# Block decay of the attention state: from a TensorE sum in every chunk, instead of a copied row past the first chunk

## The chip, the core and the metric

The kernel runs on one core of a Trainium2 chip. The metric is the device time of one execution in microseconds (us). A profiled execution gives, beside its own time, the span from the first to the last instruction of the program and a trace of every engine: PE (TensorE: matmuls; its weight loads are shown as PEld), DVE (VectorE), ACT (ScalarE), POOL (GpSimd) and SP (SyncE, whose queue issues most DMAs here).

## The reference: gated linear attention, then a soft mixture of four experts

For 4 batches and 8 heads, with sequence 768 and head size 48:

```
f = 1 / (1 + exp(-f_logit))
for t in range(S):
    state = f[:, :, t, :, None] * state + k[t] (outer) v[t]
    y[t]  = q[t] @ state
x = y with heads side by side                      # (3072, 384)
p = domain_probs / (domain_probs.sum(-1) + 1e-9)   # (3072, 4)
out = sum over 4 experts e of  p[:, e] * (relu(x @ w1[e]) @ w2[e])
```

`w1[e]` is 384x1024 and `w2[e]` 1024x384.

## The kernel before

**Tiling.** The sequence is cut into 6 chunks `c` of 128 steps. In a chunk each batch `b` has one tile with time on the 128 partitions and 8 heads by 48 channels along the rows. The recurrence is done by blocks: with `g = log(1 + exp(-f_logit))` (which is minus the log of the gate) and `cs` its running sum over the 128 steps, the scores are (q times exp(-cs)) against (k times exp(cs)), masked to the lower triangle; the state at the end of the chunk is (old state + KV) times exp(-cs of the last step). This last factor, one number for each head and channel, is the block decay, `egs`. Heads are handled in pairs: 4 pairs, each with 48 + 48 channels at partitions 0 to 47 and 64 to 111 (MP = 112 partitions).

**Steps of a chunk and batch**, with their lines:

- `gate1`, `gate2` (L247, L251): two activations on ACT give `g` in bf16, for one batch in chunk 0 and for two batches together later.
- `pe_cs` (L255): one matmul with a triangle of ones gives `cs` (128x384) in PSUM. In chunk 0 alone, L258 adds four matmuls, one for each head pair: `g` of the pair (128x112) is the stationary operand and a column of ones the moving one, so that each gives a 112x1 column with the sum of `g` over the chunk.
- `exps` (L262, L264): exp(-cs) and exp(cs) into the two halves of a tile `e`. The first is written permuted, (channel, head) instead of (head, channel). In chunk 0 alone, L266 takes the exp of the four columns into `egs` (112x4).
- `dma_egs` (L271), in chunks 1 to 4: two DMAs copy the last row of exp(-cs) onto the partitions of `egs`. The permuted order makes a channel's four pairs neighbours for this copy.
- `product` (L276): q times exp(-cs) and k times exp(cs), in bf16, on DVE or POOL.
- Transposes of q and k (on PE, L285, in chunks 0 and 1; by DMA, L289, later), scores (`pe_at`, L300), mask (`ev_at`, L304), output (`pe_y`, L311 and L315), its transpose to x (L340 on PE, or L293 by DMA).
- For the next chunk: `pe_kv` (L321), `ev_kv` (L328, DVE adds KV to the state) and `state` (L335, L336, POOL: state times `egs`, and a bf16 copy).

**The experts.** For chunk `c`, the four batches' x make 512 columns. `mm_h` (L344) does three matmuls of 512 columns for each of 8 blocks of 128 hidden units; `relu` (L350 on DVE, L352 on ACT) takes them out of PSUM; `mm_o` (L356) does four matmuls of 384 columns at a time; `ev_o` (L363, L365, L367) scales by the probability and adds. PSUM has four buffers for these (`ps_m`) and four for the attention (`ps_t`).

**What sets the order.** The program's order on each engine is written by a planner, `Plan.run` (L58): a list scheduler that is given every step with assumed costs in us, priorities, what it depends on, and the buffers ("rooms") that it takes and frees; it decides also which of the allowed engines does a step. Each engine then works in that order, whatever the real times are. The attention of chunk c + 1 is planned among the experts' work of chunk c. Between chunk 0's steps on PE it writes matmuls on a constant tile (L551, "pads"). Input loads, probability loads (`load_p`, L237, one for each chunk), `egs` copies, DMA transposes and stores all stand in SP's queue; the eight weight loads (L229) are issued by POOL, the first of them after POOL's third product and after the load of k for the last batch of chunk 0.

Of the kernel before, what the change touches and what calls it, by code (L numbers as in the profile page):

```python
# [99 lines left out]
def kernel(  # L100
# [14 lines left out]
    T = 128  # L115
# [15 lines left out]
    wk = ctx.enter_context(tc.tile_pool(name="wk", bufs=1))  # L131
    PS = bass.MemoryType.PSUM
    ps = ctx.enter_context(tc.tile_pool(name="ps", bufs=1, space=PS))
    rooms = {"ps_m": 4, "ps_t": 4, "f": 4, "q": 4, "k": 4, "v": 4, "ex": 2, "gp": 4, "e": 3, "qk": 7,
             "vb": 7, "egs": 8, "QK": 2, "AT": 2, "yb": 2, "xT": 2, "h": 2, "o": 6}
    P = Plan(rooms)


# [114 lines left out]
    def pe_cs(c, b):  # L253
        g, cs = tl("gp", c, b // 2)[:, b % 2], tl("cs", c, b)
        nc.tensor.matmul(out=cs[:, 0:HD], lhsT=Ub, rhs=g[:, :, 0:D], start=True, stop=True)  # L255
        if c == 0:
            for i in range(NP):
                nc.tensor.matmul(out=cs[0:MP, HD + i:HD + i + 1], lhsT=flat(g, i)[:, 0:MP], rhs=ones, start=True, stop=True)  # L258

    def exps(c, b):  # L260
        cs, e = tl("cs", c, b), tl("e", c, b)
        nc.scalar.activation(out=e[:, 0].rearrange("t (d h) -> t h d", d=D), in_=cs[:, 0:HD].rearrange("t (i r d) -> t r i d", r=2, d=D),  # L262
                             func=AF.Exp, scale=-1.0)
        nc.scalar.activation(out=e[:, 1], in_=cs[:, 0:HD], func=AF.Exp)  # L264
        if c == 0:
            nc.scalar.activation(out=tl("egs", c, b), in_=cs[0:MP, HD:HD + NP], func=AF.Exp, scale=-1.0)  # L266

    def dma_egs(c, b):
        last = tl("e", c, b)[T - 1:T, 0].rearrange("o (d r i) -> o r d i", r=2, d=D)
        for r in range(2):  # L270
            nc.sync.dma_start(out=tl("egs", c, b)[r * P2:r * P2 + D, :], in_=last[:, r])  # L271

    def product(c, b, j, eng):
        e = tl("e", c, b)[:, j]
        e = e.rearrange("t (d r i) -> t i r d", d=D, r=2) if j == 0 else e.rearrange("t (i r d) -> t i r d", d=D, r=2)
        engines[eng].tensor_tensor(out=tl("qk", c, b)[:, j, :, 0:D].rearrange("t (i r) d -> t i r d", r=2),  # L276
                                   in0=tl("qk"[j], c, b // 2)[:, hh(b), :].rearrange("t (i r) d -> t i r d", r=2),
                                   in1=e, op=ALU.mult)

    def cast_v(c, b, eng):  # L280
        copy(eng, tl("vb", c, b), tl("v", c, b // 2)[:, hh(b), :])
# [114 lines left out]
    xdone, kvdone = {}, {}  # L396

    def attention(c, slot, gran):
        G, X, Y, GS = {}, [], [], []
        more = c < C - 1  # L400
        for b0 in range(0, B, gran):
            p, d, half = slot(b0, 0) - 0.5, 0.54 if gran == 1 else 0.84, b0 // 2
            g1 = P.add(f"gate1 {c}.{b0}", {"ACT": d}, lambda e, b0=b0: gate1(c, b0, gran), p,
                       deps=[ld[c, "f", b0]], takes=[("ex", c, b0)], frees=[("f", c, half)])
            g2 = P.add(f"gate2 {c}.{b0}", {"ACT": d}, lambda e, b0=b0: gate2(c, b0, gran), p + 0.1,
                       deps=[g1], takes=[("gp", c, half)], frees=[("ex", c, b0)])
            for b in range(b0, b0 + gran):
                G[b] = g2
        for b in range(B):
            s = lambda k: slot(b, k)  # L410
            half = b // 2
            pt_ = lambda kind, *x: ("ps_t", kind, c, b) + x
            on = lambda f, *x: (lambda e, b=b: f(c, b, *x))
            one = lambda f, *x: (lambda e, b=b: f(c, b, *x, e))
            cs = P.add(f"cs {c}.{b}", {"PE": 0.17 if c else 0.36}, on(pe_cs), s(0),
                       deps=[G[b]], takes=[pt_("cs")], lag=0.2, frees=[("gp", c, half)])
            ex = P.add(f"exps {c}.{b}", {"ACT": 0.98 if c else 1.1}, on(exps), s(0) + 0.1, deps=[cs],
                       takes=[("e", c, b)] + ([("egs", c, b)] if c == 0 else []), frees=[pt_("cs")])
            GS.append(P.add(f"egs {c}.{b}", {"DMA": 1.0}, on(dma_egs), s(3), deps=[ex], takes=[("egs", c, b)],
                            frees=[("e", c, b)], lag=2.0) if c and more else None)  # L420
            pe = {"DVE": 0.6, "POOL": 1.0} if c < 2 else {"POOL": 1.0}
            qm = P.add(f"q {c}.{b}", pe, one(product, 0), s(4) - 0.2,
                       deps=[ex, ld[c, "q", b]], takes=[("qk", c, b)], frees=[("q", c, half), ("e", c, b)])
            km = P.add(f"k {c}.{b}", pe, one(product, 1), s(4) - 0.1,
                       deps=[ex, ld[c, "k", b]], takes=[("qk", c, b)], frees=[("k", c, half), ("e", c, b)])
            vb = P.add(f"v {c}.{b}", {"ACT": 0.52, "DVE": 0.36} if c == 0 else {"POOL": 0.5, "ACT": 0.52} if c == 1 else {"POOL": 0.5}, one(cast_v), s(4),
                       deps=[ld[c, "v", b]], takes=[("vb", c, b)], frees=[("v", c, half)])
            if c < 2:
                tq = P.add(f"tpq {c}.{b}", {"PE": 0.22}, on(pe_tp, 0), s(4), deps=[qm],
                           takes=[pt_("tp")], frees=[("qk", c, b)], lag=0.2)  # L430
                tk = P.add(f"tpk {c}.{b}", {"PE": 0.22}, on(pe_tp, 1), s(4) + 0.01, deps=[km],
                           takes=[pt_("tp")], frees=[("qk", c, b)], lag=0.2)
                et = P.add(f"ev_tp {c}.{b}", {"DVE": 0.69, "ACT": 1.05}, lambda e, b=b: copy(e, tl("QK", c, b)[0:MP], tl("tp", c, b)), s(4) + 0.1,
                           deps=[tq, tk], takes=[("QK", c, b)], frees=[pt_("tp")])
            else:
                et = P.add(f"tp {c}.{b}", {"DMA": 1.8}, on(dma_tp), s(4), deps=[qm, km], takes=[("QK", c, b)],
                           frees=[("qk", c, b)], lag=2.2)
            at = P.add(f"at {c}.{b}", {"PE": 0.35}, on(pe_at), s(7), deps=[et],
                       takes=[pt_("A", 0), pt_("A", 1)], lag=0.2, frees=[("QK", c, b)])
            eA = [P.add(f"ev_at{r} {c}.{b}", {"DVE": 0.7}, on(ev_at, r), s(7) + 0.1 + 0.1 * r, deps=[at],  # L440
                        takes=[("AT", c, b)], frees=[pt_("A", r)]) for r in range(2)]
            y = P.add(f"y {c}.{b}", {"PE": 0.4 if c else 0.28}, on(pe_y), s(11), deps=eA + [vb, kvdone.get((c - 1, b))],
                      takes=[pt_("y")], frees=[("QK", c, b), ("AT", c, b), ("vb", c, b)], lag=0.2)
            Y.append(y)
            ey = P.add(f"ev_y {c}.{b}", {"ACT": 0.48, "DVE": 0.56},
                       lambda e, b=b: copy(e, tl("yb", c, b), tl("y", c, b)[:, 0:HD]), s(11) + 0.1,
                       deps=[y], takes=[("yb", c, b)], frees=[pt_("y")])
            if c < 2:
                xt = P.add(f"xt {c}.{b}", {"PE": 0.17}, on(pe_xt), s(13), deps=[ey],
                           takes=[pt_("xp")], frees=[("yb", c, b)], lag=0.2)  # L450
                xdone[c, b] = P.add(f"ev_xt {c}.{b}", {"ACT": 0.48, "DVE": 0.4},
                                    lambda e, b=b: copy(e, tl("xT", c)[:, :, b * T:(b + 1) * T], tl("xp", c, b)),
                                    s(13) + 0.1, deps=[xt], takes=[("xT", c)], frees=[pt_("xp")])
            else:
                xdone[c, b] = P.add(f"xt {c}.{b}", {"DMA": 0.9}, on(dma_xt), s(13), deps=[ey], takes=[("xT", c)],
                                    frees=[("yb", c, b)], lag=2.2)
            X.append(xdone[c, b])
        for b in range(B if more else 0):
            on = lambda f, b=b: (lambda e: f(c, b))
            pt_ = lambda kind, b=b: ("ps_t", kind, c, b)  # L460
            s15 = slot(b, 15) if c else 2 + 2 * b
            kv = P.add(f"kv {c}.{b}", {"PE": 0.22}, on(pe_kv), s15, deps=[Y[b], X[B - 1] if c == 0 else None],
                       takes=[pt_("KV")], frees=[("vb", c, b), ("qk", c, b)], lag=0.2)
            ek = P.add(f"ev_kv {c}.{b}", {"DVE": 0.74}, on(ev_kv), s15 + 0.1,
                       deps=[kv, kvdone.get((c - 1, b))], frees=[pt_("KV")])
            kvdone[c, b] = P.add(f"state {c}.{b}", {"POOL": 1.75}, on(state), s15 + 0.2,
                                 deps=[ek, GS[b]], frees=[("egs", c, b)])


    unit = [0]  # L470
# [115 lines left out]
```

## Time and profile before

| | us |
|---|---|
| median of 3 runs | 305.13 (305.03 to 305.37) |
| the profiled execution's own time | 305.37 |
| its span | 303.5 |
| PE busy | 294.5 |
| PEld busy | 170.5 |
| ACT busy | 170.7 |
| DVE busy | 137.8 |
| POOL busy | 95.7 |

What lies around the span is 305.37 - 303.5 = 1.9 us. "Busy" of PE counts from the start of a matmul to its modelled end; matmuls overlap, so the distance from one start to the next is what a matmul costs a full PE. Groups of instructions are read as: line, engine, operation, tiles written and read, shapes, count, then busy us in total, mean ns of one, and the idle time of the engine before them with what ended it. In the timeline a row has the start in us, the length in us, and then engine, line and tiles.

### The profile page before, as it was taken

The page shows a single profiled execution, that of the slowest core. Times are in us where ns is not written, and L with a number is a line of the kernel's source. Part 1 is how long each engine was busy: PE and PEld are TensorE (multiplying, and loading weights), DVE is VectorE, ACT ScalarE, POOL GpSimd, SP SyncE. Part 2 cuts the span into 40 slices and gives each one's busy share as a digit, 9 for nine tenths or more (in the row PEclk, how much of TensorE's full clock was granted, in tenths as well). Part 3 has the DMA queues.
Part 4 walks back from the last instruction along what each step waited for, and adds up shares of the span by engine and source line. Part 5 has one row for each costly group of instructions (what it writes and reads, how often), then busy time and mean ns, then how long its engine had stood idle before and what let it go on. Part 6 is the DMA issues. An engine that isn't in the chain of part 4 may idle for free.

```text
span 303.5 us, 5499 instructions
## 1 busy us (share of the span) xinstructions
PE 294.5 (97%) x2104; PEld 170.5 (56%) x2135; DVE 137.8 (45%) x272; ACT 170.7 (56%) x295; POOL 95.7 (32%) x157
## 2 busy tenths in 40 slices
PE   7899999999999999999999999999999999999995
PEld 5665555567775655455555555555555555555552
DVE  6684013788853764516555344544423443201223
ACT  5767654957865444676356475345476444475430
POOL 4585200408656237423426243522432000000000
PEclk9999999999999999999999999999999999999999
DMA  7999999955993589776997877301322201100002
GB/s 156 204 185 208 208 206 190 225 90 91 215 208 82 111 165 181 170 144 120 189 178 136 213 142 151 51 13 37 92 59 51 48 14 41 73 5 2 0 0 104
DMA packets 137210, 36.08 MB, mean 119 GB/s; under 512 B 128480, under 2 KB 135648, under 8 KB 137184
## 3 DMA queue, kind: packets, MB, share of 16 engines
q1 hardware_dynamic: 131424, 29.45, 48.8%
q0 software_dynamic: 5760, 6.29, 12.5%
q8 instruction: 16, 0.26, 0.4%
q14 instruction: 10, 0.08, 0.1%
HBM read 31.51 MB, written 4.72 MB: 119 GB/s over the span
## 4 chain that ended last, share of the span: by engine, by line
PE 90%; DMA 4%; DVE 2%; POOL 1%; issue 1%; ACT 1%; DVEq 0%; ACTq 0%; POOLq 0%
PE ps_m L356 40%; PE ps_m L344 40%; DMA w_sb<-in_moe_w_dram 3%; PE ps_t L300 2%; PE ps_t L255 1%; PE ps_t L315 1%; PE ps_t L321 1%; PE ps_t L311 1%; PE ps_t L285 1%; DMA f<-in_f_logit_dram 1%; POOL qk L276 1%; PE ps_m L551 1%; DVE qk L276 1%; DVE o L363 0%; DVE AT L304 0%
## 5 line engine op out<-in xcount | busy, mean ns | idle before, releaser
L352 ACT ACTIVATE h<-ps_m 128x512 bf16<-128x512 f32 (+1 forms) x171 | 98.4, 578 | 102.7 <-PE ps_m L344 92.5
L356 PE MATMUL ps_m<-w_sb,h 128*128 128x384 bf16 x768 | 153.0, 326 | 0.2
L344 PE MATMUL ps_m<-xT,w_sb 128*128 128x512 bf16 (+1 forms) x593 | 150.4, 362 | 1.9 <-DVE o L367 0.3
L356 PEld LDWEIGHTS <-h 128*128 128x128 bf16 x768 | 72.5, 98 | 57.4
L363 DVE SCALAR_TENSOR_TENSOR o<-ps_m,pn,o 128x384 f32<-128x384 f32 x72 | 44.4, 617 | 97.2 <-PE ps_m L356 89.8
L344 PEld LDWEIGHTS <-w_sb 128*128 128x128 bf16 x624 | 59.8, 98 | 46.9 <-issue 0.7
L276 POOL TENSOR_TENSOR qk<-q,e 128x384 bf16<-128x384 f32 x19 | 22.8, 1203 | 66.7 <-ACT e L262 66.2
L304 DVE TENSOR_TENSOR AT<-ps_t,mask 128x512 bf16<-128x512 f32 x48 | 31.1, 685 | 19.3 <-PE ps_t L300 19.2
L335 POOL TENSOR_TENSOR Sf<-Sf,egs 48x192 f32<-48x192 f32 x40 | 20.4, 510 | 47.5 <-DVE Sf L328 45.5
L350 DVE TENSOR_SCALAR h<-ps_m 128x512 bf16<-128x512 f32 (+1 forms) x37 | 20.7, 573 | 22.0 <-PE ps_m L344 19.7
L276 POOL TENSOR_TENSOR qk<-k,e 128x384 bf16<-128x384 f32 x20 | 21.3, 1064 | 20.3 <-ACT e L264 13.0
L262 ACT ACTIVATE e<-ps_t 128x384 f32<-128x384 f32 x24 | 20.7, 864 | 4.6 <-PE ps_t L255 2.4
L328 DVE TENSOR_TENSOR Sf<-Sf,ps_t 48x192 f32<-48x192 f32 x40 | 14.0, 350 | 9.4 <-PE ps_t L321 8.7
L336 POOL CAST sb<-Sf 48x192 bf16<-48x192 f32 x40 | 13.6, 339 | 2.6
L551 PE MATMUL ps_m<-busy 128*128 128x256 bf16 x71 | 13.1, 332 | 1.3 <-DVE busy L140 1.3
L365 ACT ACTIVATE o<-ps_m,pn 128x384 f32<-128x384 f32 x20 | 11.6, 581 | 3.9 <-PE ps_m L356 3.1
L264 ACT ACTIVATE e<-ps_t 128x384 f32<-128x384 f32 x24 | 13.0, 541 | 0.0
L218 DVE CAST yb<-ps_t 128x384 bf16<-128x384 f32 x16 | 8.9, 556 | 7.3 <-PE ps_t L315 6.3
L247 ACT ACTIVATE ex<-f 128x768 f32<-128x768 f32 (+1 forms) x14 | 10.5, 747 | 3.0 <-DMA f<-in_f_logit_dram 3.0
L315 PE MATMUL ps_t<-vb,AT 128*128 128x48 bf16 x192 | 11.4, 184 | 0.7 <-DVE vb L218 0.7
L315 PEld LDWEIGHTS <-AT 128*128 128x128 bf16 x192 | 9.8, 97 | 2.8 <-issue 0.9
L251 ACT ACTIVATE gp<-ex 128x768 bf16<-128x768 f32 (+1 forms) x14 | 10.5, 751 | 0.4
(50 smaller groups left out, 142.6 us busy)
## 6 DMA issues: line engine op xcount, KB each, us to landing
w_sb<-in_moe_w_dram POOLq DMA_DIRECT2D x8, 768.0 KB, 18.6
out_dram<-o SPq DMA_DIRECT2D x24, 192.0 KB, 1.9
f<-in_f_logit_dram SPq DMA_DIRECT2D x10, 384.0 KB, 4.2
k<-in_k_dram SPq DMA_DIRECT2D x10, 384.0 KB, 5.3
q<-in_q_dram SPq DMA_DIRECT2D x10, 384.0 KB, 5.3
v<-in_v_dram SPq DMA_DIRECT2D x10, 384.0 KB, 5.5
f<-in_f_logit_dram SPq DMA_DIRECT2D x4, 192.0 KB, 3.8
k<-in_k_dram SPq DMA_DIRECT2D x4, 192.0 KB, 3.9
```

The source lines that it names most:

```text
L262: nc.scalar.activation(out=e[:, 0].rearrange("t (d h) -> t h d", d=D), in_=cs[:, 0:HD].rearrange("t (i r d) -> t r i d", r=2, d=D), func=A ...
L276: engines[eng].tensor_tensor(out=tl("qk", c, b)[:, j, :, 0:D].rearrange("t (i r) d -> t i r d", r=2), in0=tl("qk"[j], c, b // 2)[:, hh(b), ...
L304: nc.vector.tensor_tensor(out=tl("AT", c, b)[:, r].rearrange("s i t -> s (i t)"), in0=tl("A", c, b, r).rearrange("s i t -> s (i t)"), in1= ...
L315: nc.tensor.matmul(out=y[:, h * D:(h + 1) * D], lhsT=AT[:, r, i, :], rhs=vb[:, h, :], start=(c == 0), stop=True, skip_group_check=True)
L328: nc.vector.tensor_tensor(out=Sf[rows, b], in0=Sf[rows, b], in1=KV[rows, :, r, :], op=ALU.add)
L335: nc.gpsimd.tensor_tensor(out=Sf[rows, b], in0=Sf[rows, b], in1=eg, op=ALU.mult)
L344: nc.tensor.matmul(out=tl("hp", c, e, fc, n0)[:, n0:n1], lhsT=w1_sb[:, e, kk, fc * 128:(fc + 1) * 128], rhs=tl("xT", c)[:, kk, n0:n1], sta ...
L350: nc.vector.tensor_relu(out=dst, in_=src)
L352: nc.scalar.activation(out=dst, in_=src, func=AF.Relu)
L356: nc.tensor.matmul(out=tl("op", c, e, nt)[:, 0:Din], lhsT=tl("h", c, e)[:, fc, nt * T:(nt + 1) * T], rhs=w2_sb[:, e, fc, :], start=(fc == ...
L363: nc.vector.scalar_tensor_tensor(out=o, in0=op, scalar=pe, in1=o, op0=ALU.mult, op1=ALU.add)
L551: nc.tensor.matmul(out=spare[:, 0:256], lhsT=busy[:, 0:128], rhs=busy, start=True, stop=True)
```

## The change

In every chunk but the last, `pe_cs` now does the four column sums and `exps` the small exp that gives `egs`, as chunk 0 did already; the copies by DMA are gone, and with them the permuted order of exp(-cs). The products read both halves of `e` in the plain order. `e` has 2 buffers instead of 3, and the output tile `o` 8 instead of 6. The costs given to the planner are changed with it, so it writes a new order for all engines. A short description that goes with the change speaks of the domain probabilities loaded and normalised chunk by chunk; the diff leaves `load_p` and `probs` as they are, and only their places in the queues are planned anew.

```diff
     rooms = {"ps_m": 4, "ps_t": 4, "f": 4, "q": 4, "k": 4, "v": 4, "ex": 2, "gp": 4,
-             "e": 3, ... "o": 6}
+             "e": 2, ... "o": 8}
...
     def pe_cs(c, b):
...
-        if c == 0:
+        if c < C - 1:
             for i in range(NP):
                 nc.tensor.matmul(out=cs[0:MP, HD + i:HD + i + 1], lhsT=flat(g, i)[:, 0:MP], rhs=ones, start=True, stop=True)

     def exps(c, b):
         cs, e = tl("cs", c, b), tl("e", c, b)
-        nc.scalar.activation(out=e[:, 0].rearrange("t (d h) -> t h d", d=D), in_=cs[:, 0:HD].rearrange("t (i r d) -> t r i d", r=2, d=D),
-                             func=AF.Exp, scale=-1.0)
+        nc.scalar.activation(out=e[:, 0], in_=cs[:, 0:HD], func=AF.Exp, scale=-1.0)
         nc.scalar.activation(out=e[:, 1], in_=cs[:, 0:HD], func=AF.Exp)
-        if c == 0:
+        if c < C - 1:
             nc.scalar.activation(out=tl("egs", c, b), in_=cs[0:MP, HD:HD + NP], func=AF.Exp, scale=-1.0)

-    def dma_egs(c, b):
-        last = tl("e", c, b)[T - 1:T, 0].rearrange("o (d r i) -> o r d i", r=2, d=D)
-        for r in range(2):
-            nc.sync.dma_start(out=tl("egs", c, b)[r * P2:r * P2 + D, :], in_=last[:, r])
-
     def product(c, b, j, eng):
-        e = tl("e", c, b)[:, j]
-        e = e.rearrange("t (d r i) -> t i r d", d=D, r=2) if j == 0 else e.rearrange("t (i r d) -> t i r d", d=D, r=2)
-        engines[eng].tensor_tensor(out=tl("qk", c, b)[:, j, :, 0:D].rearrange("t (i r) d -> t i r d", r=2),
-                                   in0=tl("qk"[j], c, b // 2)[:, hh(b), :].rearrange("t (i r) d -> t i r d", r=2),
-                                   in1=e, op=ALU.mult)
+        engines[eng].tensor_tensor(out=tl("qk", c, b)[:, j, :, 0:D], in0=tl("qk"[j], c, b // 2)[:, hh(b), :],
+                                   in1=tl("e", c, b)[:, j].rearrange("t (h d) -> t h d", d=D), op=ALU.mult)
...
-            cs = P.add(f"cs {c}.{b}", {"PE": 0.17 if c else 0.36}, on(pe_cs), s(0),
+            cs = P.add(f"cs {c}.{b}", {"PE": 0.36 if more else 0.17}, on(pe_cs), s(0),
                        deps=[G[b]], takes=[pt_("cs")], lag=0.2, frees=[("gp", c, half)])
-            ex = P.add(f"exps {c}.{b}", {"ACT": 0.98 if c else 1.1}, on(exps), s(0) + 0.1, deps=[cs],
-                       takes=[("e", c, b)] + ([("egs", c, b)] if c == 0 else []), frees=[pt_("cs")])
-            GS.append(P.add(f"egs {c}.{b}", {"DMA": 1.0}, on(dma_egs), s(3), deps=[ex], takes=[("egs", c, b)],
-                            frees=[("e", c, b)], lag=2.0) if c and more else None)
+            ex = P.add(f"exps {c}.{b}", {"ACT": 1.1}, on(exps), s(0) + 0.1, deps=[cs],
+                       takes=[("e", c, b)] + ([("egs", c, b)] if more else []), frees=[pt_("cs")])
...
             kvdone[c, b] = P.add(f"state {c}.{b}", {"POOL": 1.75}, on(state), s15 + 0.2,
-                                 deps=[ek, GS[b]], frees=[("egs", c, b)])
+                                 deps=[ek], frees=[("egs", c, b)])
```

More of the change, by code (lines that the diff above doesn't have):

```diff
@@ L133 @@
     ps = ctx.enter_context(tc.tile_pool(name="ps", bufs=1, space=PS))
-    rooms = {"ps_m": 4, "ps_t": 4, "f": 4, "q": 4, "k": 4, "v": 4, "ex": 2, "gp": 4, "e": 3, "qk": 7,
-             "vb": 7, "egs": 8, "QK": 2, "AT": 2, "yb": 2, "xT": 2, "h": 2, "o": 6}
+    rooms = {"ps_m": 4, "ps_t": 4, "f": 4, "q": 4, "k": 4, "v": 4, "ex": 2, "gp": 4, "e": 2, "qk": 7,
+             "vb": 7, "egs": 8, "QK": 2, "AT": 2, "yb": 2, "xT": 2, "h": 2, "o": 8}
     P = Plan(rooms)
@@ L398, in attention @@
     def attention(c, slot, gran):
-        G, X, Y, GS = {}, [], [], []
+        G, X, Y = {}, [], []
         more = c < C - 1
```

## The prediction, made before the changed kernel was run

> **What bounds the kernel now.** I read the page first: shares of the engines, clock, and the chain that ended last.
>
> ```profile
> span 303.5 us, 5499 instructions
> ...
> PE 294.5 (97%) x2104; PEld 170.5 (56%) x2135; DVE 137.8 (45%) x272; ACT 170.7 (56%) x295; POOL 95.7 (32%) x157
> ...
> PEclk9999999999999999999999999999999999999999
> ...
> PE 90%; DMA 4%; DVE 2%; POOL 1%; issue 1%; ACT 1%; DVEq 0%; ACTq 0%; POOLq 0%
> ```
>
> PE is busy 97% of the span at full granted clock, and 90% of the chain is PE; the next engine is at 56%. But busy PE is not yet full PE, so next come PE's waits for other engines, over the whole span:
>
> ```profile
> PE ps_t L315 <- DVE vb L218: 0.7, 1, 0.7
> ...
> PE ps_m L344 <- DVE o L367: 0.3, 1, 0.3
> PE ps_t L285 <- DVE qk L276: 0.3, 1, 0.3
> ```
>
> The first of these lies at 15 us, in the opening. From the first expert matmul at 23.04 us on, the two others are all: about 0.65 us in 276. So from there on PE is the bound in the strict sense: what is added to its queue is added to the time, and a faster ACT, DVE, POOL or SP buys at most those 0.65 us. Before 23.04 us PE is not the bound. The chain of waits, in order of time, shows what is (start, length, what):
>
> ```profile
> 13.60 1.31 POOL qk L276
> 14.91 8.08 DMA w_sb<-in_moe_w_dram
> 22.99 0.04 issue
> 23.04 0.39 PE ps_m L344
> ```
>
> POOL's third product must end before POOL issues the first weight load, the load takes 8.08 us, and the first expert matmul starts 0.05 us after it lands. Here ACT's and POOL's speed does count.
>
> **Part 1, added: four column sums in chunks 1 to 4.** 4 chunks by 4 batches are 16 groups of four matmuls (64, each with its weight load of 112 columns), on the engine that is the bound. The price is read from chunk 0, which has such groups. PE's timeline:
>
> ```profile
> 12.66 0.33 PE L255 MATMUL ps_t<-gp,Ub 128*128 128x384 bf16 x1
> 12.82 0.32 PE L258 MATMUL ps_t<-ones,gp 128*112 128x1 bf16 x4
> 13.01 0.27 PE L551 MATMUL ps_m<-busy 128*128 128x256 bf16 x1
> ```
>
> From the start of the group to the start of the next matmul: 13.01 - 12.82 = 0.19 us, with nothing waited for. 16 x 0.19 = 3.04 us. The 0.32 us of length are no price: they overlap what follows. Bounds: above, four matmuls with 112-column weights and 96 moving columns (`pe_kv`), in the steady state, take 63.58 - 63.38 = 0.20 us, 3.2 in all:
>
> ```profile
> 63.38 0.36 PE L321 MATMUL ps_t<-vb,qk 128*112 128x96 bf16 x4
> 63.58 0.81 PE L356 MATMUL ps_m<-w_sb,h 128*128 128x384 bf16 x4
> ```
>
> Below, eight matmuls with 128-column weights and 48 moving columns go in 18.16 - 17.94 = 0.22 us, that is 0.11 for four, 1.76 in all:
>
> ```profile
> 17.94 0.37 PE L315 MATMUL ps_t<-vb,AT 128*128 128x48 bf16 x8
> 18.16 0.60 PE L551 MATMUL ps_m<-busy 128*128 128x256 bf16 x4
> ```
>
> I take 3.04, the row of the very instruction. The groups in the steady state stand between the same kinds of neighbour (a 384-column L255 before, a matmul with 128-column weights behind).
>
> That the weight load sets this price is told by PEld's groups: L321 x80 at a mean of 131 ns and L258 x16 at 170 for 112 columns, against L356 x768 at 98 for 128 columns; the narrower load is the slower. The Trainium skill, "TensorE: Matmul & The Clock Gate", section "Weight-path perf modes — Fast Weight Load (FWL) and DoubleRow", has a rule for it: the fast load is on when the number of weights is 128, so 112 columns do without. Its section "LDWEIGHTS (loading the stationary operand)" then gives P / 1.2 ns for P columns, 93 ns for 112; if every load stood in the open, the 64 would cost 6.0 us and the prediction would be some 3 us higher. The group's row, 190 ns for four loads, is half of that, so the measurement decides and the sum goes by 3.04.
>
> **Part 2, in the opening: exp(-cs) in plain order.** ACT's groups:
>
> ```profile
> L262 ACT ACTIVATE e<-ps_t 128x384 f32<-128x384 f32 x24 | 20.7, 864 | 4.6 <-PE ps_t L255 2.4 <-PE ps_t L258 2.3
> L264 ACT ACTIVATE e<-ps_t 128x384 f32<-128x384 f32 x24 | 13.0, 541 | 0.0
> L266 ACT ACTIVATE egs<-ps_t 112x4 f32<-112x4 f32 x4 | 0.7, 165 | 0.0
> ```
>
> The permuted exp takes 864 ns, the plain one 541. Consecutive activations overlap: from 9.28 (L262) to 9.93 (L264) are 0.65 us, from 9.93 to 10.36 (L266) 0.43, so a plain one brings what follows on ACT forward by 0.22 us. Two lie on the chain: `exps` of batch 1 starts at 9.28 because its cs has just ended on PE, which does not move (pads stand before it, and their number, 71, is the same in the new program). From there ACT works without a hole up to `exps` of batch 2 at 12.36. Its cs ends on PE near 12.05 and stays there, since three pads from 10.97 lead up to it; brought forward by 0.22, `exps` starts at 12.14, still behind it. With its own 0.22, POOL's third product starts 0.44 us earlier, and the weight load is issued at 14.47. Its other condition, k of batch 3, had landed at 14.31. So the issue gains 0.4 us. The load of 8.08 us shares the DMA engines with inputs until 18.0, so its end gains between 0 and 0.44; nothing stands ahead of it in POOL's own queue, and DMA moved least just when it ramped up (103 GB/s between 17 and 18 us, 138 in the next, against 241 at 15 and 209 at 20), so I take 0.4. The other thing that the first expert matmul waits for, x of batch 3, is copied from 22.44 to 22.92 and must gain as much: on DVE, which runs without a hole from 9.79, the permuted q products cost 11.17 - 10.40 = 0.77 each against 16.77 - 16.30 = 0.47 for a plain one, three of them 0.9; enough. `e` with 2 buffers makes batch 2's exps wait for batch 0's products, which ended at 7.4 and 8.3: nothing.
>
> **Part 3, work that moves or goes beside PE.** ACT loses 24 x 0.323 = 7.8 us of length and gains 16 x 0.165 = 2.6; POOL's q products fall from 1203 ns toward the 1064 of k; SP loses 32 issues of a median of 578 ns (18.5 us) and the waits before them, so the loads of chunk 2 are no longer behind the copies of chunk 1's decays and start near 61 us instead of 71.6. None of this had PE waiting but for the two waits of 0.3 us, both about chunk 1, where DVE's permuted q product and an o scaling were late and where ACT was filled by chunk 2's permuted exps. In the new order chunk 2's first cs stand before the 512-column halves there, so both waits can go, and new ones can come: the stretch takes relus of 256 columns (388 ns on ACT) as fast as PE makes them. From -0.65 (both gone) to +1.0 (three waits of the largest kind, 0.35 us); I take -0.35, half gone. POOL never waited for a copied `egs` (its 45.5 us at L335 are all for DVE), so an earlier one gives nothing. The probability loads: chunk 1's is issued earlier, those of 2 and 3 one behind the other; each lands in about 2.8 us, chunks ahead of its use.
>
> The added wait is the `e` slot: `exps` of a batch waits for both products, mostly on POOL, of the batch two before. Behind it on ACT stand relus, and behind these PE, when its four `ps_m` buffers are full. The planner places exps by assumed product costs of 1.0 us, real ones take 1.06, so lateness of a tenth of a microsecond is to be expected, less than the gap of 0.7 us that ACT shows before most relus of the steady state. I cost it at nothing; without that cover it is the second rival.
>
> **Sum.** 3.04 - 0.4 - 0.35 = +2.3 us. The profiled execution, 305.37 (span 303.5 and 1.9 around it), becomes 307.7; it was the slowest of the three runs, 0.24 above the median, so against 305.13 I predict 307.4.
>
> **Rivals.**
>
> - *The opening gives nothing.* DMA is full until 18.0 us and the first weights land when the bytes are through; or x is late. For it: DMA stands at the top tenth from the second of the 40 slices to the eighth. Against: the dip between 17 and 19 us, room that an earlier issue can use. Then +3.04 - 0.35 to +3.04: 307.8 to 308.2.
> - *ACT's head is held by the `e` slot.* Decides where exps' wait exceeds the 0.7 us before relus. A product of 1.2 us late, less 0.7, in each of chunks 1 to 4: 4 x 0.5 = 2.0 on top, 309.4. Against: POOL is 32% busy.
> - *Faster: the sums hide.* If the 112-column loads slip wholly under the neighbours' streams, a group costs nothing and the opening and the freed waits remain: -0.75, 304.4. It decides below 0.75 / 16 = 0.047 us for a group. Against: 0.19 in the row above, with PE not waiting, and 0.11 even for the cheapest four.
> - *The change does not do what its short description says*: the probabilities' loads only move in the queue, which is worth nothing either way; the time is then that of parts 1 to 3.
>
> **How the numbers follow.** The forecast (+1.4 to +2.7: 306.5 to 307.8) has 0.63; no gain in the opening 0.17; the `e` slot or another new wait of that size 0.12; cheaper sums (0.11 a group, 1.76 - 0.75 = +1.0, 306.1) 0.04; hidden sums 0.04. The range, 306.2 to 308.7, holds the first two and part of the third. A measurement of this kernel tells about 0.2% (0.6 us) from no change: faster 0.03, same 0.04 (the bottom of the last two cases), slower 0.93.
>
> **What would show it.** 80 matmuls in the column-sum group, 64 of them new, at 0.18 to 0.20 us for four in the steady timeline; exp(-cs) at 541 ns; the first weight load issued near 14.5 and the first expert matmul near 22.6 us; PE's waits after it together below 1 us; the end of PE's work about 2.3 us later. It is wrong if a group costs another time among the experts' matmuls, if the first expert matmul does not move, or if PE waits for relus behind an exps.

## The result, and the profile after

The changed kernel takes 308.91 us (median of 4 runs, 308.25 to 308.97) against 305.10 for the kernel before: 3.8 us slower, a ratio of 1.0118 (95% interval 1.0101 to 1.0136). The direction was forecast; the size was not: 307.4 was predicted, with a range that ended at 308.7.

In some executions, of the kernel before and of changed ones alike, PE loses 5 to 11 us ahead of the first expert matmul to one late input load; the medians and ratios below leave them out, and where a profile fell into one (`changed_again`, `sums_128_wide`, `opening_kept`) only its rows behind the opening are read.

The page of the changed kernel: span, engines, and the head of the chain that ended last.

```profile
span 307.1 us, 5567 instructions
...
PE 297.0 (97%) x2168; PEld 173.5 (56%) x2199; DVE 134.8 (44%) x268; ACT 166.3 (54%) x316; POOL 90.5 (29%) x156
...
PE 89%; DMA 4%; SPq 3%; DVE 1%; issue 1%; DVEq 0%
```

PE remains the bound. ACT and POOL have less to do, as forecast, and it buys nothing. PE's waits for other engines, over the whole span:

```profile
...
PE ps_m L335 <- DVE o L358: 1.2, 1, 1.2
PE ps_t L306 <- DVE vb L218: 0.8, 2, 0.5
PE ps_m L335 <- DMA w_sb<-in_moe_w_dram: 0.6, 1, 0.6
PE ps_t L255 <- ACT gp L251: 0.4, 1, 0.4
```

Before, the two waits behind the opening were 0.3 us each; now there is one of 1.17, the first line, for the o scaling in DVE's queue near 83 us, and just ahead of it one of 0.14 for a relu, too short for the list; the other three lines are of the opening. The column sums, PE's groups by shape:

```profile
L258 PE MATMUL ps_t<-ones,gp 128*112 128x1 bf16 x80 | 6.8, 188 | 0.0
```

80 matmuls instead of 16, and PE waited for none of them. The opening, by the chain in order of time:

```profile
10.51 3.88 DMA k<-in_k_dram
14.39 0.30 issue
14.70 8.51 DMA w_sb<-in_moe_w_dram
23.20 0.05 issue
23.25 0.39 PE ps_m L335
```

POOL's product is no longer in it: the load of k is, which landed at 14.39, and the weight load followed 0.3 us later. So the issue came 0.21 us earlier than before (14.70 for 14.91), but the load took 8.5 us instead of 8.1, and the first expert matmul starts at 23.25 instead of 23.04. POOL's third product ended at 14.27 here; it was not what the issue waited for.

**Where the time went.** Two points of PE's timeline split the kernel: the first running sum of chunk 1 (L255), at 54.43 us before and 54.53 after, and PE's last end, 299.96 and 303.54. Up to the first point the change costs 0.10 us; from there on 249.006 - 245.532 = 3.47. The start-to-start distances of the 64 new sums add to 2.93 (28 ns for the first matmul in a group, 52 for each of the next three); PE's waits went from 0.64 (0.295 + 0.347) to 1.31 us (1.166 + 0.143), 0.67 more. 2.925 + 0.667 = 3.59; the 0.12 too much lies in PE's other work, whose order the new plan changes, and was not followed further.

### The profile page after: what moved, and what is told of

Its sections match the earlier page's. It is cut to its first block, busy times and chain, and to the rows that moved or that the text cites. A ratio compares the mean times of both kernels' runs of the same rounds, so it can differ in the third digit from the quotient of the medians.

```text
span 307.1 us, 5567 instructions
## 1 busy us (share of the span) xinstructions
PE 297.0 (97%) x2168; PEld 173.5 (56%) x2199; DVE 134.8 (44%) x268; ACT 166.3 (54%) x316; POOL 90.5 (29%) x156
## 4 chain that ended last, share of the span: by engine, by line
PE 89%; DMA 4%; SPq 3%; DVE 1%; issue 1%; DVEq 0%
PE ps_m L347 41%; PE ps_m L335 40%; SPq L222 3%; DMA w_sb<-in_moe_w_dram 3%; PE ps_t L291 2%; PE ps_t L312 1%; PE ps_t L306 1%; DMA k<-in_k_dram 1%; PE ps_t L302 1%; PE ps_t L255 1%; PE ps_t L258 1%; PE ps_t L276 1%; DVE o L354 0%; DVE psm L242 0%; DVE Sf L319 0%
## 5 line engine op out<-in xcount | busy, mean ns | idle before, releaser
L343 ACT ACTIVATE h<-ps_m 128x512 bf16<-128x512 f32 (+1 forms) x173 | 99.9, 577 | 109.7 <-PE ps_m L335 100.2
L268 POOL TENSOR_TENSOR qk<-q,e 128x384 bf16<-128x384 f32 x18 | 18.2, 1016 | 59.6 <-ACT e L262 57.3
L341 DVE TENSOR_SCALAR h<-ps_m 128x512 bf16<-128x512 f32 (+1 forms) x35 | 19.4, 567 | 23.5 <-PE ps_m L335 23.0
L356 ACT ACTIVATE o<-ps_m,pn 128x384 f32<-128x384 f32 x22 | 12.8, 580 | 5.1 <-PE ps_m L347 3.3
L262 ACT ACTIVATE e<-ps_t 128x384 f32<-128x384 f32 x24 | 11.7, 489 | 4.1 <-PE ps_t L258 4.1
L218 POOL CAST vb<-v 128x384 bf16<-128x384 f32 x18 | 9.5, 541 | 12.4 <-DMA v<-in_v_dram 7.0
L263 ACT ACTIVATE e<-ps_t 128x384 f32<-128x384 f32 x24 | 11.9, 497 | 0.0
```

The costliest lines, as they stand in the source:

```text
L268: engines[eng].tensor_tensor(out=tl("qk", c, b)[:, j, :, 0:D], in0=tl("qk"[j], c, b // 2)[:, hh(b), :], in1=tl("e", c, b)[:, j].rearrange( ...
L341: nc.vector.tensor_relu(out=dst, in_=src)
L343: nc.scalar.activation(out=dst, in_=src, func=AF.Relu)
L356: nc.scalar.activation(out=o, in_=op, func=AF.Copy, scale=pe)
```

## What ran into what near 82 us

DVE in the changed kernel, around the wait (start, length, what):

```profile
81.23 0.17 DVE L241 TENSOR_REDUCE psm<-pt 128x4 f32<-128x16 f32 x1
81.43 0.97 DVE L242 TENSOR_SCALAR psm<-psm 128x4 f32<-128x4 f32 x1
82.44 0.18 DVE L243 RECIPROCAL psm<-psm 128x4 f32<-128x4 f32 x1
82.66 0.20 DVE L244 TENSOR_TENSOR pn<-pt,psm 128x16 f32<-128x16 f32 x1
82.89 0.62 DVE L358 TENSOR_SCALAR o<-ps_m,pn 128x384 f32<-128x384 f32 x1
```

and POOL at the same time:

```profile
80.43 1.00 POOL L268 TENSOR_TENSOR qk<-q,e 128x384 bf16<-128x384 f32 x1
81.38 1.00 POOL L268 TENSOR_TENSOR qk<-k,e 128x384 bf16<-128x384 f32 x1
```

This is the normalisation of chunk 1's probabilities. Adding 1e-9 to 128x4 numbers, 0.17 us in the kernel before, took 0.97 and ended at 82.40, 0.02 after POOL's second product. In the kernel before, the same four operations stood at 80.34 to 81.17, and POOL's products of chunk 2 began at 81.86:

```profile
80.54 0.17 DVE L242 TENSOR_SCALAR psm<-psm 128x4 f32<-128x4 f32 x1
...
81.86 1.19 POOL L276 TENSOR_TENSOR qk<-q,e 128x384 bf16<-128x384 f32 x1 [0.32 <-POOL sb L336]
...
81.87 3.37 PE L344 MATMUL ps_m<-xT,w_sb 128*128 128x256 bf16 x27 [0.35 <-DVE o L367]
```

The new plan has chunk 2's exps earlier, so the two products come earlier too, between the states of chunk 1, and the normalisation now falls on them. The o scaling that frees a `ps_m` buffer stands behind it in DVE's queue, and PE waits for that buffer, for 1.17 us:

```profile
83.56 2.67 PE L335 MATMUL ps_m<-xT,w_sb 128*128 128x256 bf16 x23 [1.17 <-DVE o L358]
```

The Trainium skill, "SBUF — State Buffer", section "Who interferes with whom", says that a pair of ports is shared by VectorE and GpSimd as an exclusive lock: a DVE operation with two SBUF inputs (against a GpSimd instruction that reads SBUF), or a `tensor_scalar` in a mode that uses both ports, waits until the GpSimd instruction that holds the pair is over; a `tensor_reduce` does not. The rows agree: the `tensor_scalar` was held, and the reduce, which began at 81.23 inside POOL's first product, was not. In which mode the `tensor_scalar` ran, the trace does not show.

## The experiments

**The sums alone.** The kernel before with only this change (its `egs` still come by DMA):

```diff
-        if c == 0:
+        if c < C - 1:
             for i in range(NP):
                 nc.tensor.matmul(out=cs[0:MP, HD + i:HD + i + 1], lhsT=flat(g, i)[:, 0:MP], rhs=ones, ...)
```

> The kernel before, in its own order on every engine, with the four column sums added to the running sum's step in chunks 1 to 4; nothing reads them. Theory (each group costs PE 0.18 us wherever it stands, because from 23 us on PE is full): 16 groups, +2.9 us, 308.0 (307.7 to 308.3), with PE's waits as before. Rival (the sums are partly hidden and the rest of the 3.8 us of the change is the new order): 306.5 or less.

Measured: 307.79 us, ratio 1.0073 (1.0060 to 1.0086), some 2.2 us. The sums' distances in the trace add to 2.93, as in the changed kernel. From chunk 1's running sum to PE's end it was 248.03 - 245.53 = 2.50 us more. Of PE's two waits that had been there before, one had gone and the other was 0.10 us; the lines below are of the opening alone:

```profile
...
PE ps_m L344 <- DMA w_sb<-in_moe_w_dram: 0.8, 1, 0.8
PE ps_t L315 <- DVE vb L218: 0.7, 1, 0.7
PE ps_t L255 <- ACT gp L251: 0.5, 1, 0.5
```

What follows: work added to PE gives the others time, so part of it is paid for by PE's own waits, here some 0.5 us of the 0.64. The price of a group is what the opening's row said, wherever the group stands.

**The changed kernel without the new sums.** The counterpart: the order of the changed kernel, with `if c == 0` back in `pe_cs` and the small exp reading four columns of the running sum, so that the block decay of chunks 1 to 4 is left out.

> The changed kernel in its own order, without the column sums of chunks 1 to 4: the small exp reads four columns of the running sum instead, so the block decay of these chunks is left out. Theory: 308.9 - 2.9 = 306.0, that is 0.9 above the kernel before, which is the part of opening (+0.2) and of the waits near 82 us (+0.6). Rival (the new order costs most): 307 or more.

Measured: 305.54, ratio 1.0009 (0.9987 to 1.0031): no different from the kernel before by the times, and 1.09% below the changed kernel's 1.0118, some 3.3 us. From chunk 1's running sum to PE's end it was 245.81, 0.28 more than before and 3.20 less than the changed kernel: 2.93 of sums and, as the wait near 82 us was 0.93 instead of 1.17, 0.24 of wait. (The addition came ahead of POOL's second product here and took 0.23 us; the multiplication behind it was held, for 0.70.) So the sums are the bulk, and the new order itself costs 0.3 us, not the 0.9 expected.

**Without the addition of 1e-9.** In the changed kernel:

```diff
-        nc.vector.tensor_single_scalar(out=s, in_=s, scalar=1e-9, op=ALU.add)
```

> The changed kernel without the addition of 1e-9 to the sum of the probabilities (that part of the normalisation is left out). Theory: that operation of DVE took 0.97 us instead of 0.17 in chunk 1 because POOL's two products ran then, and PE waited for the o scaling behind it. Without it PE's wait of 1.17 us near 83 us falls to about 0.4 and the time to 308.1. Rival (DVE is held by POOL whatever it does, so the reciprocal or the multiplication takes over the wait): 308.9, and one of these at about 0.9 us.

Measured: 308.46, ratio 1.0091 (1.0077 to 1.0105), between the theory's 308.1 and the rival's 308.9. DVE's rows:

```profile
81.19 0.17 DVE L241 TENSOR_REDUCE psm<-pt 128x4 f32<-128x16 f32 x1
81.39 0.18 DVE L242 RECIPROCAL psm<-psm 128x4 f32<-128x4 f32 x1
81.61 0.77 DVE L243 TENSOR_TENSOR pn<-pt,psm 128x16 f32<-128x16 f32 x1
82.41 0.62 DVE L357 TENSOR_SCALAR o<-ps_m,pn 128x384 f32<-128x384 f32 x1
```

The rival's mechanism: the hold passed to the multiplication, with two SBUF inputs, which ended at 82.38, 0.03 after POOL's product (81.35 + 1.00). The reciprocal, begun at 81.39 inside that product, was not held. The scaling started at 82.41 instead of 82.89 only because two operations fewer stood behind the hold, and PE's wait fell to 0.73 us, not to 0.4.

**The normalisation moved away from the products.** In the changed kernel, behind the plan:

```diff
     done = P.run()
+    names = [o.name for o in done]
+    early = done.pop(names.index("probs 1"))
+    done.insert(names.index("ev_at0 1.2"), early)
```

> The changed kernel with one thing moved: DVE normalises chunk 1's probabilities before the masks of chunk 1's third batch (about 73 us) instead of after its last x (81 us), so that its operations meet none of POOL's two products; the order of PE, ACT, POOL and SP is unchanged. Theory: the o scaling behind it starts at 81.3 instead of 82.9 and PE's wait of 1.17 us near 83 us falls below 0.3: 0.9 to 1.2 us less than the changed kernel. Rival (relus on DVE and ACT are the next in line and take the wait over): no gain, 0.3 us or less.

Measured: 307.23, ratio 1.0064 (1.0051 to 1.0078), against 1.0125 (1.0110 to 1.0140) for the changed kernel in the same group of runs. From chunk 1's running sum to PE's end: 247.68 against 249.02, 1.34 us less, a little more than expected and 1.18 of it the wait; the times say 1.9, and where the rest lies was not followed. PE's list of waits has nothing of DVE's scaling any more:

```profile
PE ps_t L255 <- ACT gp L251: 1.5, 4, 0.6
...
PE ps_t L276 <- DVE qk L268: 0.8, 1, 0.8
PE ps_m L335 <- DMA w_sb<-in_moe_w_dram: 0.6, 1, 0.6
PE ps_t L331 <- ACT yb L216: 0.3, 1, 0.3
```

The addition takes 0.17 us there:

```profile
74.33 0.17 DVE L242 TENSOR_SCALAR psm<-psm 128x4 f32<-128x4 f32 x1
```

This shows what PE waited for: the same four operations on the same data, 7 us earlier, and the wait is gone. The move takes away the hold and the operations' own length at that place together. By the rows the hold is 0.97 - 0.17 = 0.80 us of the 1.17; without it, by that estimate, 0.37 would stay, as much as the 0.35 of the kernel before. The rival, relus taking the wait over, fell.

**The changed kernel again.**

> The changed kernel once more, as the base of this group of runs and as a second look at its opening. Theory: the 3.6 us are lasting parts (2.9 sums, 0.7 the wait near 83 us) and the start of the first expert matmul varies by some 0.5 us from execution to execution with the landing of the first weights, without moving the end by as much: 3.2 to 3.8 us above the kernel before. Rival (the opening's 0.2 us is a lasting loss): the first expert matmul at 23.2 again.

Measured: 308.97, ratio 1.0125 (1.0110 to 1.0140). Its profile has the wait near the o scaling again, 1.18 us, with the addition at 0.99 us, and 249.02 us from chunk 1's running sum to the end. It does not show the opening; other profiles do. First expert matmul in the old opening: 23.04 (`before`), 23.75 (`sums_alone`) and 22.69 (`before_mended`, below); in the new one: 23.25, 23.13 (`no_new_sums`), 22.65 (`no_add`), 22.59 (`probs_early`) and 23.35 (`changed_mended`, below). The 0.2 us of the changed kernel's profile are scatter, not a lasting loss.

The same profiles show what sets the issue of the first weight load. In all eight profiles with the new opening that are read there, POOL issues it 0.30 us after k of the last batch has landed (landing 14.10 to 14.45, issue 14.40 to 14.75), and its third product had ended before. In the old opening the product set it in `before` and `sums_alone` (issue 14.91 and 14.94), but not in `before_mended`, where the issue came at 14.66, again 0.30 us behind k. There PE ran its second running sum at 7.82 us in 0.32 us, against 0.53 us at 8.43 in `before`, and the third product, for all its permuted exps, ended at 14.23. So the plain exps bring the issue forward in some executions only, and then by some 0.3 us.

**The sums' weights 128 columns wide.**

```diff
-                nc.tensor.matmul(out=cs[0:MP, HD + i:HD + i + 1], lhsT=flat(g, i)[:, 0:MP], rhs=ones, ...)
+                nc.tensor.matmul(out=cs[:, HD + i:HD + i + 1], lhsT=flat(g, i), rhs=ones, ...)
```

> The changed kernel with the column sums' stationary operand 128 columns wide instead of 112 (the 16 more are the zeros that pad each head to 64), otherwise as it is. Theory (the load of 112 columns sets the 51 ns from one sum to the next, and one of 128 columns is faster, as the 28 ns between the 48-column matmuls with 128-column weights say): a group falls from 0.18 to 0.11 us, 16 x 0.07 = 1.2 us less than the changed kernel. Rival (51 ns is what a matmul of one column with its load costs, whatever the width): no difference, or 14% more per load, +0.4 us.

Measured: 307.39, ratio 1.0071 (1.0057 to 1.0084), 0.54% or 1.6 us below the changed kernel of the same group. PEld's group first in the changed kernel:

```profile
L258 PEld LDWEIGHTS <-gp 128*112 128x112 bf16 x80 | 7.6, 138 | 2.7 <-issue 0.7
```

and here, with PE's timeline below it:

```profile
L258 PEld LDWEIGHTS <-gp 128*128 128x128 bf16 x80 | 4.8, 97 | 4.8 <-issue 2.3
```

```profile
83.67 0.24 PE L258 MATMUL ps_t<-ones,gp 128*128 128x1 bf16 x4
83.77 0.38 PE L312 MATMUL ps_t<-vb,qk 128*112 128x96 bf16 x4
```

A group takes 0.10 us from start to start instead of 0.18; the distances of the 64 add to 1.65 us instead of 2.93, 25 ns where there were 52. Most of the other 0.3 us is the wait for the o scaling, which was 0.82 here: the addition came 0.04 us ahead of POOL's second product and took 0.17, and the multiplication was held instead, for 0.65. So the column sum's price is the load of its weights, and a wider load is the cheaper one. The rule cited in the prediction (the Trainium skill, "TensorE: Matmul & The Clock Gate", section "Weight-path perf modes — Fast Weight Load (FWL) and DoubleRow": the fast load is on when the number of weights is 128) agrees with this. The 93 ns for 112 columns that the formula of its section "LDWEIGHTS (loading the stationary operand)" gives are not what a load costs in the stream here, where a load and its matmul take 52.

**The opening, three ways.** First, the changed kernel with chunk 0's probabilities behind the first weight load:

```diff
-        nc.sync.dma_start(out=p_dst[:, :, c], in_=p_src[:, :, c])
+        i = nc.sync.dma_start(out=p_dst[:, :, c], in_=p_src[:, :, c])
+        if c == 0:
+            after(i, ins["w", 0])
```

> The changed kernel with chunk 0's probability load held back until the first weight load has landed. Theory: in the changed kernel the 512 short packets of that load went between the packets of the first weight load and cost it 0.4 us; without them the weights land 8.1 us after their issue, at 22.8, and the first expert matmul starts at 22.85 instead of 23.25: 308.5. Rival (the bytes of the inputs before it set the landing): 23.2 again, 308.9.

Measured: 308.98, ratio 1.0117 (1.0097 to 1.0137), no gain, although the weights landed at 22.55 and the first expert matmul started at 22.59. That the probabilities' packets had cost the weights 0.4 us is not shown, as `no_add` and `probs_early` got there with these packets in place. What the three have in common is what came after. The first running sum of chunk 1, in `probs_early` (ACT's gates and PE's sum):

```profile
52.57 0.84 ACT L247 ACTIVATE ex<-f 128x768 f32<-128x768 f32 x1 [1.74 <-DMA f<-in_f_logit_dram]
...
53.45 0.84 ACT L251 ACTIVATE gp<-ex 128x768 bf16<-128x768 f32 x1
...
54.34 0.32 PE L255 MATMUL ps_t<-gp,Ub 128*128 128x384 bf16 x1 [0.31 <-ACT gp L251]
```

PE waits for the gates, whose input had just landed. From the first expert matmul to this sum PE has 31.28 us of work (in the changed kernel, `sums_alone` and `no_new_sums` alike, with no wait there). The gates end between 53.9 and 54.8 us in the eleven profiles read there, and an earlier start of PE does not bring them forward: so a first expert matmul earlier than about 22.6 to 23.6, by where the gates end in that execution, is given back here. Even the kernel before stood at this floor:

```profile
53.53 0.84 ACT L251 ACTIVATE gp<-ex 128x768 bf16<-128x768 f32 x1
...
54.43 0.48 PE L255 MATMUL ps_t<-gp,Ub 128*128 128x384 bf16 x2
```

Its gates ended at 54.37 and its sum began 0.05 us later, the same distance as in `probs_early`, `no_add`, `p0_behind_w0` and `plain_opening`, where PE waits for them. From the first expert matmul to the sum it took 31.39 us, so 0.11 us of it was a wait that the list does not show.

Second, the opening's part of the change by itself, in the kernel before:

```diff
+        if c == 0:
+            nc.scalar.activation(out=e[:, 0], in_=cs[:, 0:HD], func=AF.Exp, scale=-1.0)
...
+        if c == 0:
+            engines[eng].tensor_tensor(out=tl("qk", c, b)[:, j, :, 0:D], in0=tl("qk"[j], c, b // 2)[:, hh(b), :],
+                                       in1=e.rearrange("t (h d) -> t h d", d=D), op=ALU.mult)
+            return
```

> The kernel before, in its own order, with exp(-cs) and its product in plain order in chunk 0 alone: the opening's part of the change by itself. Theory: the weight load is issued 0.2 to 0.4 us earlier, but PE cannot keep it, because chunk 1's running sum waits near 54.4 us for gates whose load is fixed by the weight loads: within 0.2 us of the kernel before (ratio 0.9993 to 1.0007). Rival (what the prediction said): 0.4 us less, 0.9987.

Measured: 305.30, ratio 1.0004 (0.9992 to 1.0015). The weight load was issued at 14.44 instead of 14.91. That is the prediction's 14.47 by luck: the product ended at 13.20, and the issue followed k, which landed at 14.14 in this execution. The first expert matmul started at 22.92, and PE gave it back:

```profile
54.76 0.48 PE L255 MATMUL ps_t<-gp,Ub 128*128 128x384 bf16 x2 [0.40 <-ACT gp L251]
```

Third, to keep the gain: as the first, with chunk 1's first gate load started one weight load earlier.

```diff
         if (c, nm, b) == (1, "f", 0):
-            after(ins[c, nm, b], ins["w", 5])
+            after(ins[c, nm, b], ins["w", 4])
+        if (c, nm, b) == (1, "k", 0):
+            after(ins[c, nm, b], ins["w", 5])
```

> The changed kernel with chunk 0's probabilities behind the first weight load, and chunk 1's first gate load started after the fifth weight load instead of the sixth (the loads behind it still wait for the sixth). Theory: a first expert matmul at 22.6 is given back at 54 us because the running sum of chunk 1 waits there for gates whose load ends at 52.4, fixed by the weight loads before it; with that load some 4 us earlier the gain stays: no wait of PE for ACT near 54 us, and 0.5 us less than the changed kernel. Rival (nothing is lost at 54 us): the time of the kernel that only held the probabilities back, which was that of the changed kernel.

Measured: 309.04, ratio 1.0136 (1.0118 to 1.0154): nothing gained. Its profile does not show the opening, so the kernel ran once more.

> The kernel of opening_kept once more, for a profile to read. Theory: chunk 1's first gates are ready near 51 us instead of 54.3, PE has no wait for ACT at its running sum, and this sum starts 31.3 us after the first expert matmul. Rival: the earlier load pushes the seventh weight load back, and PE waits for that one or for another load instead.

Measured: 308.71 (one run). SP's row of the load, and then ACT's and PE's:

```profile
38.02 0.37 SPq L222 DMA_DIRECT2D f<-in_f_logit_dram  x1
```

```profile
52.65 0.84 ACT L251 ACTIVATE ex<-f 128x768 f32<-128x768 f32 x1 [1.58 <-DMA f<-in_f_logit_dram]
...
54.42 0.32 PE L259 MATMUL ps_t<-gp,Ub 128*128 128x384 bf16 x1
```

My expectation fell: issued 4.3 us earlier than in the changed kernel (42.29), the load landed no earlier, at 52.62 against 52.28. The DMA records suggest why: as long as weights are on their way, the load's 192-byte packets go one for one with the weights' packets, some 190 a microsecond each (43 to 50 us), and only when the weights have nearly gone do they run at 1100 a microsecond. The weights lose by it: the last of their loads landed at 52.43 instead of 51.36, and the gate load 0.2 us behind it. This points to what both queues have to move, and not to the issue, as what sets the end; no run changed the bytes to show it. So the floor stands, and how to lower it stays open.

**Versions with these mendings.** The kernel before, with the normalisation of chunk 1 moved in the same way and the state update's weights widened:

```diff
-            nc.tensor.matmul(out=tl("KV", c, b)[0:MP, i * 2 * D:(i + 1) * 2 * D], lhsT=flat(kp, i)[:, 0:MP],
+            nc.tensor.matmul(out=tl("KV", c, b)[:, i * 2 * D:(i + 1) * 2 * D], lhsT=flat(kp, i),
```

> The kernel before (decays by DMA), in its own order, with chunk 1's probabilities normalised earlier on DVE, and the stationary operand of the state update's matmuls 128 columns wide instead of 112. Theory: 80 matmuls at 42 instead of 52 ns (-0.8), and the wait of 0.35 us near 82 us gone: 304.0, about 1.1 us less than the kernel before. Rival (the 96 moving columns and not the load set the 52 ns; another wait follows): 304.8 or more.

Measured: 304.71, ratio 0.9983 (0.9973 to 0.9993): faster than both, but against the kernel before by half of what was expected. The widening did its part, 0.6 us instead of the 0.8 expected: the 80 matmuls' distances fall to 3.42 us, 43 ns each instead of 52, from 4.04 in `plain_opening`, which has the same order on PE. (In the trace of the kernel before they add to 4.25, since the record of a matmul behind one group is missing and its 0.22 us count as the group's.) One group here:

```profile
62.94 0.33 PE L321 MATMUL ps_t<-vb,qk 128*128 128x96 bf16 x4
63.11 0.81 PE L356 MATMUL ps_m<-w_sb,h 128*128 128x384 bf16 x4
```

But the wait of 0.35 us near 82 us was replaced by a longer one, for ACT:

```profile
82.87 1.36 PE L344 MATMUL ps_m<-xT,w_sb 128*128 128x256 bf16 x11 [0.62 <-ACT h L352]
```

Here the second half of the rival held: with DVE's scaling out of the way, a relu behind ACT's permuted exps of chunk 2 was next.

The changed kernel with all three mendings:

> The changed kernel with the same two mendings and the column sums 128 wide. Theory: 1.6 us less by the probabilities, 1.3 by the sums and 0.8 by the state update: 305.2, still 1.2 us above the kernel before with its mendings, since the sums (now 1.65 us) remain on PE. Rival (with its waits gone the changed kernel is no worse than the mended one before): 304.5 or less.

Measured: 305.59, ratio 1.0032 (1.0006 to 1.0059). From chunk 1's running sum to PE's end: 245.89 us, 3.1 less than the changed kernel and 0.86 more than `before_mended` (245.03): its 1.65 us of sums, less the waits that the other one still has (0.91 us against 0.14). So with its waits gone the changed form is still the slower.

## Why the prediction was wrong in size, by its own steps

- **Part 1, the sums (+3.04): right.** 2.93 by the trace; the row from the opening, 0.19 us for a group, held in the steady state (0.183), and that the width of the load sets it is now shown (`sums_128_wide`) and not only argued.
- **Part 2, the opening (-0.4): the step that failed first.** It had two conditions wrong. The issue: the step saw that k of batch 3 had landed at 14.31 and put 14.47 behind it, but POOL issues 0.30 us after k's landing, so that 0.3 us was the most to be gained, and only where the product is late; it came at 14.70. The end: the step stopped at the first expert matmul and took what comes after for free of other conditions. Matmuls at 22.6 to 22.9 occurred, but with the old opening too (22.69), and the gain cannot pass chunk 1's running sum, whose gates end near 54.3 us; the kernel before already waited there, 0.11 us by the working above. Worth 0 (`plain_opening`: ratio 1.0004); the changed kernel's profile has +0.10 at that point. The profile of before had told it: its gate row ended at 54.37 and the sum started at 54.43, and I had looked only for waits that PE was charged with.
- **Part 3, the waits (-0.35): the wrong sign.** They went from 0.64 to 1.31 us, +0.67, inside the bounds given (-0.65 to +1.0) but far from the value taken, so that the error of this step alone is 1.0 us. I looked at what ACT and DVE would do in the new order and costed the probabilities' normalisation at nothing, since its loads land in time. What it met was POOL: the addition took 0.97 us instead of 0.17, and PE stood for 1.17.
- **The `e` slot: right to cost at nothing.** In the changed kernel's profile no exps, and no relu behind them, waits for a product.
- **The sum:** 3.04 - 0.4 - 0.35 = 2.3 against 3.58 at PE's end (3.5 between the two profiled executions): sums -0.11, opening +0.5, waits +1.02, other order -0.12. Two rivals had a part of it each, the one without the opening's gain and the one of a new wait, though that one looked for it on ACT and not on DVE; I had no case in which both hold. With the waits as measured, 305.13 + 3.04 + 0.67, such a case gives 308.8.

## What to carry to other kernels

Where one engine is full, price what is added to it by the distance from start to start in the same stage, and do not count as gain what the next wait down the line, even one too short for the list of waits, will take back: find the first later point that is tied to a load. When a plan is written anew, look at what small operations of VectorE will meet on GpSimd, not only at which engine is free. And give a stationary operand 128 columns, zeros included, where the matmuls on it are short: 25 ns instead of 52 for a sum of one column, 43 instead of 52 for 96 columns.

## What the runs showed of the hardware that I had not expected

- A DVE `tensor_scalar` on 128x4 numbers took 0.97 to 0.99 us instead of 0.17 in all five traces in which POOL's 128x384 product had started 0.03 to 0.05 us before it; a `tensor_tensor` with two SBUF inputs was held in the same way (0.65 to 0.77 for 0.18 in `no_add`, `no_new_sums` and `sums_128_wide`), a reduce and a reciprocal were not. A cast on POOL does it too: 0.38 us at 128.75 in `sums_alone`, ending 0.02 after the cast.
- Two DMA queues shared by packets and not by bytes in `opening_kept_2`: 190 packets of 192 bytes a microsecond beside as many of the weights, whose packets carried 768 bytes there, so that a load of short packets went at a sixth of the 1100 a microsecond that it reached behind them (issue 4.3 us earlier, landing 0.3 us later).
- Exp in plain order took 489 ns in the changed kernel and its neighbour 497, where the neighbour of the permuted one had taken 541.
